# Two parts of the first block's input: from GpSimd's converting loads to SyncE's float32 loads and GpSimd's casts, with w_out's load moved

## The chip, the cores and the metric

The kernel runs on one core of a Trainium2 chip. The core has five engines that run side by side, each with its own instruction queue: TensorE (PE in the profile), VectorE (DVE), ScalarE (ACT), GpSimd (POOL) and SyncE (SP). TensorE loads weights (PEld) and multiplies. SyncE does no arithmetic here; it issues DMA transfers, as ScalarE and GpSimd also can. All transfers run on the core's 16 DMA engines; those that GpSimd issues stand in queue q0 of the profile, those of SyncE in q1. The metric is the device time of one run in microseconds (us).

## The reference

The reference first smooths the input along the sequence with a causal filter of 7 taps, one filter for each of 8 heads with softmax-normalized taps, and then applies a two-layer network with a leaky ReLU:

```python
w = weight - np.max(weight, axis=-1, keepdims=True)          # 8 heads x 7 taps
w = np.exp(w)
w = w / (np.sum(w, axis=-1, keepdims=True) + 1e-09)
x_pad = np.concatenate([np.zeros((B, 6, D)), x], axis=1)     # x: 8 x 4096 x 192
idx = np.arange(S)[:, None] + np.arange(7)[None, :]
x_unf = x_pad[:, idx, :].reshape(B, S, 7, 8, 24)
y = np.einsum('hk,bskhg->bshg', w, x_unf).reshape(B * S, D)  # 32768 x 192
h = y @ w_in                                                 # 192 x 2048
g = np.maximum(0.01 * h, h)
out = g @ w_out                                              # 2048 x 192
```

Inputs and output are float32. The kernel computes with bfloat16 operands.

## The kernel before

The tokens are taken in 32 blocks: a block is 512 positions of two sequences (e = 0 and 1), whose 64-channel chunks lie in the two halves of the partitions. The first two blocks are cut into halves of 256 positions, called groups 0 to 3; from then on a group is a whole block. For a group, the smoothed input yt is made in the layout channels by positions (mostly on DVE: one L222 and six L228 instructions a chunk), TensorE multiplies it with w_in into ph (L507), ScalarE applies the leaky ReLU and writes g (L515), and TensorE multiplies g with w_out (L525 in the first groups, L588 later). The instructions on each engine stand in the order in which the code is written (a manual schedule); waits between engines follow from the tiles that they share.

The channels-by-positions layout needs x transposed. Blocks from 2 on are loaded by GpSimd with conversion to bfloat16 (load_x, L96) and transposed by a DMA that SyncE issues (L114). The four parts (256 positions each) of the first two blocks go other ways, since they are wanted at once:

- Part 0 is loaded in float32 by SyncE (x_nat, L142), cast into x_half by ScalarE and VectorE (cast_first, L155), transposed on TensorE (L181) and copied from there into xt.
- Parts 1 and 2 (called the second and third part) are loaded by GpSimd with conversion into x_rows (load_first, L145), transposed on TensorE (transpose_first, L167; twelve small matmuls that write the tile ptr) and copied into xt by VectorE (evac_first, L195). The first of the two transposes stands in TensorE's order inside group 0's first L507 batch, behind 8 matmuls; the second stands in group 0 ahead of its last batch.
- Part 3 is loaded by GpSimd with conversion into x_half (L149) and transposed by SyncE's DMA (L199).

GpSimd's order of issue before the change: w_in0 for rows 0 to 127; the constant ident; w_in0 for the other 64 rows, in two column halves called near and far, with the two loads of part 1 between them; w_in1 in two loads; the two loads of part 2; w_out in two loads (L350); two small operations that make the filter taps wk (L445, L446), which every L222 and L228 reads; the six loads of part 3; and then the blocks of load_x. w_in's rows are also copied between the halves of the partitions by VectorE and ScalarE (spread_up L326, spread_down L322) before TensorE can use them.

The helper sync adds a wait by hand: its first argument waits for its second. The pool that holds the float32 tile x_nat has two buffers.

Of the kernel before, what the change touches and what calls it, by code (L numbers as in the profile page):

```python
# [10 lines left out]
FP32 = mybir.dt.float32  # L11
BF16 = mybir.dt.bfloat16
# [3 lines left out]
def kernel(  # L16
# [8 lines left out]
    nc = tc.nc  # L25

    B, S, D = x.shape
# [13 lines left out]
    HS = SUB // 2  # L41
    NFC = F // 128
# [3 lines left out]
    RUN = 4  # L46
# [10 lines left out]
    const_pool = ctx.enter_context(tc.tile_pool(name="const", bufs=1))  # L57
    stage_pool = ctx.enter_context(tc.tile_pool(name="stage", bufs=2))
# [17 lines left out]
    x_nat, x_bf, xt = {}, {}, {}  # L76

    def sync(after, first, why):
        tc.add_manual_dep(
            after.ins, first.ins.name,  # L80
            mybir.DependencyInfo(
                mybir.DependencyClass.Sync, mybir.DependencyReason.DATA
            ),
            reason=why,
        )

    def load_x(blk, after=None):

        if blk >= NBLK:
            return  # L90
        rp, st = divmod(blk, NB)
        t = xb_pool.tile([128, NCH, SUB, 2, CH], BF16, name="x_bf")
        src = x[:, st * ST : (st + 1) * ST, :].rearrange("r (s p) d -> r p s d", p=128)
        for c in range(NCH):
            for e in range(2):
                ins = nc.gpsimd.dma_start(  # L96
                    out=t[:, c, :, e, :],
                    in_=src[2 * rp + e, :, :, c * CH : (c + 1) * CH],
                )
                if after is not None:  # L100
                    sync(ins, after, "behind a nearer block's transposes")
                    after = None
        x_bf[blk] = t
# [18 lines left out]
    def new_xt(rp):  # L122
        xt[rp] = xt_pool.tile([128, NCH, HALO + S], BF16, name="xt")
        nc.vector.memset(xt[rp][:, :, 0:HALO], 0.0)
# [8 lines left out]
    x_rows = {  # L133
        q: const_pool.tile([128, 2, HS, D], BF16, name=f"x_rows{q}") for q in (1, 2)
    }

    def load_first(q):
        rows = x[0:2, q * HT : (q + 1) * HT, :].rearrange("e (s p) d -> p e s d", s=HS)
        if q == 0:
            x_nat[q] = stage_pool.tile([128, 2, HS, D], FP32, name="x_nat")  # L140
            for s in range(HS):
                nc.sync.dma_start(out=x_nat[q][:, :, s], in_=rows[:, :, s])  # L142
        elif q in x_rows:
            for e in range(2):
                nc.gpsimd.dma_start(out=x_rows[q][:, e], in_=rows[:, e])  # L145
        else:
            for c in range(NCH):
                for e in range(2):
                    nc.gpsimd.dma_start(  # L149
                        out=x_half[q][:, c, :, e, :],  # L150
                        in_=rows[:, e, :, c * CH : (c + 1) * CH],
                    )

    def cast_first(q, s, copy, e=slice(0, 2)):
        copy(  # L155
            out=x_half[q][:, :, s, e, :],
            in_=x_nat[q][:, e, s, :].rearrange("p e (c k) -> p c e k", c=NCH),
        )
# [76 lines left out]
    def y_of(grp, c):  # L235
        blk, t0, T = grp
        if blk not in yt:
            yt[blk] = yt_pool.tile([128, NCH, ST], BF16, name="yt")
        return yt[blk][:, c, t0 : t0 + T]
# [47 lines left out]
    w9 = const_pool.tile([H, K + 1], FP32, name="w9")  # L287
    nc.scalar.dma_start(out=w9[:, 0:K], in_=weight)  # L288
    load_first(0)

    ones = nc.const_aps.tensor(1.0, [128, ST], BF16)
# [7 lines left out]
    for sign, off in ((1, 0), (-1, GRP - 1)):  # L299
        nc.gpsimd.affine_select(  # L300
            out=sel[:, :, 0, :], in_=sel[:, :, 0, :], compare_op=mybir.AluOpType.is_ge,
# [12 lines left out]
    def load_w_in(n, rows, cols=slice(0, WF)):  # L314
        ps, slot = ((0, 128), 0) if rows == 0 else ((0, CH), 2)
        nc.gpsimd.dma_start(  # L316
            out=w_in[n][ps[0] : ps[1], slot, cols],
            in_=moe_w_in[rows : rows + ps[1], n * WF + cols.start : n * WF + cols.stop],
        )
# [17 lines left out]
    ident = const_pool.tile([128, 128], BF16)  # L337
    make_identity(nc, ident)
    load_w_in(0, 128, near)
    load_first(1)  # L340
    load_w_in(0, 128, far)
    for rows in (0, 128):
        load_w_in(1, rows)
    load_first(2)


    w_out = const_pool.tile([128, NFC, D], BF16)
    for h in range(2):
        cs = slice(h * NFC // (2 * RUN), (h + 1) * NFC // (2 * RUN))
        nc.gpsimd.dma_start(  # L350
            out=w_out.rearrange("p (c i) d -> p c i d", i=RUN)[:, cs],
            in_=moe_w_out.rearrange("(c p i) d -> p c i d", p=128, i=RUN)[:, cs],
        )


    wa = psum_h.tile([128, 2, ST], FP32, name="warm", tag="ph")
# [1 line left out]
    def warm(n, cols=HT, to=wa[:, 0]):  # L358
# [10 lines left out]
        out=nmax, in_=w9[:, 0:K], axis=mybir.AxisListType.X,  # L369
# [3 lines left out]
        out=w9[:, 0:K], in_=w9[:, 0:K], func=mybir.ActivationFunctionType.Exp,  # L373
# [18 lines left out]
    def select(out, parts):  # L392
# [9 lines left out]
    select(wps_hm, slice(0, 2))  # L402
    wps_hm = wps_hm[:, :, 0]
    new_xt(0)
    cast_first(0, 0, nc.scalar.copy)
    cast_first(0, 1, nc.scalar.copy, slice(0, 1))
    cast_first(0, 1, nc.vector.tensor_copy, slice(1, 2))
    taps = const_pool.tile([128, NCH, 2, K + 1, 2], BF16, name="taps")
    nc.vector.tensor_copy(
        out=taps, in_=wps_hm[..., None].to_broadcast([128, NCH, 2, K + 1, 2])  # L410
# [5 lines left out]
    def diag_wide(c, p):  # L416
# [22 lines left out]
        out=rsum, in0=wml[:, :, K:], scalar=1e-9, in1=taps[:, :, 0, K:, 0],  # L439
# [4 lines left out]
    wk = const_pool.tile([128, NCH, K], FP32, name="wk")  # L444
    nc.gpsimd.tensor_add(wk, taps[:, :, 0, 0:K, 0], wml[:, :, 0:K])  # L445
    nc.gpsimd.tensor_mul(wk, wk, rsum.to_broadcast([128, NCH, K]))  # L446
    load_first(3)
    load_x(2)
    diag_wide(1, 1)
# [4 lines left out]
    def act_scale(out, in_, scale):  # L454
# [11 lines left out]
        out=y_of(groups[0], 0), in0=hi[:, :HT], scalar=rsum[:, 0, :], in1=low,  # L466
# [301 lines left out]
```

## Time and profile before

| | |
|---|---|
| median of 3 runs | 680.97 us (680.66 to 681.43) |
| profiled execution, span from its first to its last instruction | 679.2 us |
| what the median has beyond that span | 1.8 us |
| TensorE busy | 674.9 us, 99% of the span, at the full granted clock |
| VectorE, ScalarE, GpSimd busy | 71%, 76%, 22% |
| first L507 matmul | 8.09 us |
| transpose of x's second and third part on TensorE | 8.65 us and 15.98 us |
| first matmul with w_out (L525) | 17.12 us |

The profile gives one execution; its own time is known as the span, and the 1.8 us that the median of the runs has beyond it lie before its first and after its last instruction or are differences between executions. TensorE works almost without a pause from 8.09 us to the end, so the time is decided by what happens ahead of that, by short pauses behind it, and by the amount of TensorE's work, which the change leaves alone. In lists of instructions a line reads: start, duration, engine, line of the code, operation, output tile <- input tiles, count, and in brackets the idle time ahead of it with what ended it.

### The profile page before, as it was taken

The numbers are of one execution on the slowest core, as the hardware profiler recorded it, in microseconds if no ns is written. First come the engines' busy times: TensorE is split into PE (matmuls) and PEld (weight loads), VectorE is DVE, ScalarE is ACT, GpSimd is POOL, SyncE is SP. The second block draws the span as 40 slices with busy tenths as digits, with TensorE's granted clock in tenths as the row PEclk, the third lists the DMA queues.
The fourth block names the chain that finished last, engine by engine and source line by source line (L and its number), as shares of the span: only waits on it lengthen the run. The fifth ranks groups of instructions, "written<-read, shape, count | busy, mean of one in ns | idle before, by whom it ended". The sixth has DMA issues, their size and how long they took to land.

```text
span 679.2 us, 27092 instructions
## 1 busy us (share of the span) xinstructions
PE 674.9 (99%) x12442; PEld 446.3 (66%) x12442; DVE 481.2 (71%) x816; ACT 517.6 (76%) x601; POOL 147.4 (22%) x208
## 2 busy tenths in 40 slices
PE   9999999999999999999999999999999999999998
PEld 6997666666666666666666666666666666666667
DVE  7989477866768766778667687667786676876612
ACT  7899877777787777777777777778777777777781
POOL 8455221122211222211222112222022220000000
PEclk9999999999999999999999999999999999999999
DMA  9999755655737656556556566567365573321123
GB/s 149 99 119 104 52 85 83 84 64 67 96 74 93 76 54 86 84 85 86 66 63 92 80 92 78 56 83 94 73 87 69 60 96 71 72 56 33 34 49 94
DMA packets 213970, 53.27 MB, mean 78 GB/s; under 512 B 209312, under 2 KB 213536, under 8 KB 213856
## 3 DMA queue, kind: packets, MB, share of 16 engines
q0 software_dynamic: 98832, 13.97, 30.3%
q1 hardware_dynamic: 115008, 37.57, 28.0%
q8 instruction: 97, 1.59, 0.9%
q14 instruction: 17, 0.14, 0.1%
q10 hardware_dynamic: 16, 0.00, 0.0%
HBM read 28.31 MB, written 25.17 MB: 79 GB/s over the span
## 4 chain that ended last, share of the span: by engine, by line
PE 98%; DVE 1%; ACT 0%; issue 0%; ACTq 0%
PE ph L507 49%; PE acc L588 44%; PE po L525 5%; PE acc L259 0%; DVE diag L420 0%; PE ptr L167 0%; ACT L366 0%; ACTq L288 0%; DVE w_in L322 0%; DVE yt L465 0%; DVE o_sb L638 0%; DVE x_half L155 0%; ACT w L372 0%; DVE w_in L326 0%; ACT junk L366 0%
## 5 line engine op out<-in xcount | busy, mean ns | idle before, releaser
L515 ACT ACTIVATE g<-ph 128x1024 bf16<-128x1024 f32 x512 | 496.6, 1021 | 139.8 <-PE ph L507 139.6
L228 DVE SCALAR_TENSOR_TENSOR yt<-xt,wk,yt 128x512 bf16<-128x512 bf16 (+1 forms) x582 | 380.1, 715 | 0.2
L507 PE MATMUL ph<-yt,w_in 64*64 64x512 bf16 (+2 forms) x6048 | 377.5, 369 | 0.3 <-DVE yt L465 0.3
L588 PE MATMUL acc<-g,w_out 64*64 64x512 bf16 x5568 | 339.9, 376 | 0.0
L507 PEld LDWEIGHTS <-w_in 64*64 64x64 bf16 (+1 forms) x6048 | 229.7, 131 | 103.4 <-issue 1.1
L588 PEld LDWEIGHTS <-w_out 64*64 64x64 bf16 x5568 | 178.2, 118 | 118.8
L96 POOL DMA_DIRECT2D x_bf<-in_x_dram x180 | 133.9, 774 | 407.6 <-DMA xt<-x_bf 405.6
L610 DVE STREAM_TRANSPOSE o_t<-acc 128x512 f32<-128x512 f32 x87 | 72.9, 875 | 182.2 <-PE acc L588 182.2
L525 PE MATMUL po<-w_out,g 64*128 64x192 bf16 (+1 forms) x640 | 36.8, 243 | 0.0
L525 PEld LDWEIGHTS <-g 64*128 64x128 bf16 (+1 forms) x640 | 32.6, 95 | 3.2 <-issue 0.4
L222 DVE TENSOR_SCALAR yt<-xt,wk 128x512 bf16<-128x512 bf16 (+1 forms) x97 | 28.8, 320 | 2.4 <-DMA xt<-x_bf 2.4
L598 ACT COPY junk<-junk 128x1 f32<-128x1 f32 x58 | 11.1, 191 | 4.1
L638 DVE COPY o_sb<-po 128x192 f32<-128x192 f32 x8 | 2.8, 356 | 6.8 <-PE po L525 3.9
L638 ACT COPY o_sb<-po 128x192 f32<-128x192 f32 x16 | 5.1, 323 | 0.3
L259 PE MATMUL acc<-xt,diag 64*64 64x256 bf16 x126 | 4.7, 272 | 0.1
L149 POOL DMA_DIRECT2D x_half<-in_x_dram x6 | 4.3, 732 | 0.9 <-DMA w_in<-in_moe_w_in_dram 0.9
L259 PEld LDWEIGHTS <-diag 64*64 64x64 bf16 x140 | 3.7, 106 | 1.0 <-issue 0.4
L360 PE MATMUL warm<-const-bfloat16-1.0 128*128 128x512 bf16 (+2 forms) x8 | 3.3, 577 | 0.8 <-PEq L752 0.8
L145 POOL DMA_DIRECT2D x_rows<-in_x_dram x4 | 2.9, 746 | 0.0
L316 POOL DMA_DIRECT2D w_in<-in_moe_w_in_dram x5 | 2.9, 593 | 0.0
L360 PEld LDWEIGHTS <-const-bfloat16-1.0 128*128 128x128 bf16 x10 | 1.2, 128 | 2.2 <-issue 2.2
L326 DVE COPY w_in<-w_in 64x512 bf16<-64x512 bf16 (+1 forms) x7 | 2.3, 337 | 0.2
(52 smaller groups left out, 25.9 us busy)
## 6 DMA issues: line engine op xcount, KB each, us to landing
out_dram<-o_t SPq DMA_DIRECT2D x112, 192.0 KB, 4.7
x_bf<-in_x_dram POOLq DMA_DIRECT2D x180, 64.0 KB, 3.1
out_dram<-o_sb SPq DMA_DIRECT2D x8, 192.0 KB, 2.8
xt<-x_bf SPq DMA_TRANSPOSE x90, 3.2
w_out<-in_moe_w_out_dram POOLq DMA_DIRECT2D x2, 384.0 KB, 8.3
out_dram<-o_t SPq DMA_DIRECT2D x8, 96.0 KB, 2.4
out_dram<-o_sb SPq DMA_DIRECT2D x8, 96.0 KB, 1.7
w_in<-in_moe_w_in_dram POOLq DMA_DIRECT2D x2, 256.0 KB, 5.5
```

Source lines behind the costliest of these rows:

```text
L96: ins = nc.gpsimd.dma_start(out=t[:, c, :, e, :], in_=src[2 * rp + e, :, :, c * CH : (c + 1) * CH],)
L222: lambda s=src, d=dst, c=c: nc.vector.tensor_scalar_mul(d, s, wk[:, c, 0:1])
L228: lambda s=src, d=dst, c=c, k=k: nc.vector.scalar_tensor_tensor(out=d, in0=s, scalar=wk[:, c, k : k + 1], in1=d, op0=mybir.AluOpType.mult, ...
L259: lambda k=k, p=p, a=a, ps=ps, to=to, acc=accs[e]: nc.tensor.matmul(out=acc[to, :T], lhsT=diag[c][ps, p, k, :], rhs=xt[0][ps, c, a : a + T ...
L360: nc.tensor.matmul(out=to[:, 0:cols], lhsT=ones[:, 0:128], rhs=ones[:, 0:cols], start=True, stop=True,)
L507: nc.tensor.matmul(out=ph[m : m + M, e, i * T : (i + 1) * T], lhsT=w_in_of(f, e, c, m, m + M), rhs=y[ps, c, t0 : t0 + T], start=(c == chun ...
L515: act = nc.scalar.activation(out=g[blk][:, nf * u : nf * (u + 1), :, t0 : t0 + T], in_=ph.rearrange("p e (i t) -> p i e t", i=nf), func=my ...
L525: return nc.tensor.matmul(out=po[m], lhsT=g[b][ps, fc, e, s * 128 : (s + 1) * 128], rhs=w_out[ps, fc, :], start=start, stop=stop,)
L588: ins = nc.tensor.matmul(out=acc2[gi, r][e * CH : (e + 1) * CH, 0:T], lhsT=w_out_of(ps, fc, r), rhs=g[b][ps, fc, e, t0 : t0 + T], start=fi ...
L598: seal = nc.scalar.copy(out=junk, in_=junk)
L610: nc.vector.transpose(out=osb[gi, 0][:, 0 : T // GB, :, r], in_=acc2.pop((gi, r))[:, 0:T].rearrange("p (j k) -> p j k", k=GB),)
L638: ins = copy(out=o_sb[:, n % 2, :], in_=po.pop(n))
```

## The change

The second and the third part of x are no longer loaded with conversion by GpSimd. SyncE loads each in float32 into a tile x_nat, in two transfers, and GpSimd casts each into x_rows with two copies. SyncE's loads of the second part wait for ScalarE's first cast of part 0; those of the third part wait for GpSimd's second cast of the second part. On GpSimd, w_out's two loads now stand behind the casts of the second part, and ahead of everything of the third; wk's two operations follow, then the casts of the third part, then the loads of part 3 and of the blocks as before. What TensorE, VectorE and ScalarE execute, and its order, is the same in both kernels. SyncE has four more loads ahead of its first DMA transpose.

```diff
--- before.py
+++ after.py
@@ -134,12 +134,18 @@
         q: const_pool.tile([128, 2, HS, D], BF16, name=f"x_rows{q}") for q in (1, 2)
     }
 
-    def load_first(q):
+    def load_first(q, after=None):
         rows = x[0:2, q * HT : (q + 1) * HT, :].rearrange("e (s p) d -> p e s d", s=HS)
         if q == 0:
             x_nat[q] = stage_pool.tile([128, 2, HS, D], FP32, name="x_nat")
             for s in range(HS):
                 nc.sync.dma_start(out=x_nat[q][:, :, s], in_=rows[:, :, s])
+        elif q in (1, 2):
+            x_nat[q] = stage_pool.tile([128, 2, HS, D], FP32, name="x_nat")
+            for e in range(2):
+                ins = nc.sync.dma_start(out=x_nat[q][:, e], in_=rows[:, e])
+                if e == 0:
+                    sync(ins, after, "behind a nearer part")
         elif q in x_rows:
             for e in range(2):
                 nc.gpsimd.dma_start(out=x_rows[q][:, e], in_=rows[:, e])
@@ -152,7 +158,7 @@
                     )
 
     def cast_first(q, s, copy, e=slice(0, 2)):
-        copy(
+        return copy(
             out=x_half[q][:, :, s, e, :],
             in_=x_nat[q][:, e, s, :].rearrange("p e (c k) -> p c e k", c=NCH),
         )
@@ -337,20 +343,9 @@
     ident = const_pool.tile([128, 128], BF16)
     make_identity(nc, ident)
     load_w_in(0, 128, near)
-    load_first(1)
     load_w_in(0, 128, far)
     for rows in (0, 128):
         load_w_in(1, rows)
-    load_first(2)
-
-
-    w_out = const_pool.tile([128, NFC, D], BF16)
-    for h in range(2):
-        cs = slice(h * NFC // (2 * RUN), (h + 1) * NFC // (2 * RUN))
-        nc.gpsimd.dma_start(
-            out=w_out.rearrange("p (c i) d -> p c i d", i=RUN)[:, cs],
-            in_=moe_w_out.rearrange("(c p i) d -> p c i d", p=128, i=RUN)[:, cs],
-        )
 
 
     wa = psum_h.tile([128, 2, ST], FP32, name="warm", tag="ph")
@@ -402,9 +397,20 @@
     select(wps_hm, slice(0, 2))
     wps_hm = wps_hm[:, :, 0]
     new_xt(0)
-    cast_first(0, 0, nc.scalar.copy)
+    after = cast_first(0, 0, nc.scalar.copy)
+    load_first(1, after)
     cast_first(0, 1, nc.scalar.copy, slice(0, 1))
     cast_first(0, 1, nc.vector.tensor_copy, slice(1, 2))
+    for e in range(2):
+        gate = nc.gpsimd.tensor_copy(out=x_rows[1][:, e], in_=x_nat[1][:, e])
+    w_out = const_pool.tile([128, NFC, D], BF16)
+    for h in range(2):
+        cs = slice(h * NFC // (2 * RUN), (h + 1) * NFC // (2 * RUN))
+        nc.gpsimd.dma_start(
+            out=w_out.rearrange("p (c i) d -> p c i d", i=RUN)[:, cs],
+            in_=moe_w_out.rearrange("(c p i) d -> p c i d", p=128, i=RUN)[:, cs],
+        )
+    load_first(2, gate)
     taps = const_pool.tile([128, NCH, 2, K + 1, 2], BF16, name="taps")
     nc.vector.tensor_copy(
         out=taps, in_=wps_hm[..., None].to_broadcast([128, NCH, 2, K + 1, 2])
@@ -444,6 +450,8 @@
     wk = const_pool.tile([128, NCH, K], FP32, name="wk")
     nc.gpsimd.tensor_add(wk, taps[:, :, 0, 0:K, 0], wml[:, :, 0:K])
     nc.gpsimd.tensor_mul(wk, wk, rsum.to_broadcast([128, NCH, K]))
+    for e in range(2):
+        nc.gpsimd.tensor_copy(out=x_rows[2][:, e], in_=x_nat[2][:, e])
     load_first(3)
     load_x(2)
     diag_wide(1, 1)
```

## The prediction

> **What bounds the kernel now.** I read the page's busy times first, then the chain that ended last, then its first microseconds, then the DMA packets.
>
> ```profile
> PE 674.9 (99%) x12442; PEld 446.3 (66%) x12442; DVE 481.2 (71%) x816; ACT 517.6 (76%) x601; POOL 147.4 (22%) x208
> ...
> PE 98%; DVE 1%; ACT 0%; issue 0%; ACTq 0%
> ```
>
> TensorE is dense: 98% of the chain is PE. The only room is the ramp ahead of the first L507 matmul at 8.09 us and a few short gaps behind it. The chain in order of time shows the place that the change touches:
>
> ```profile
> 7.56 0.49 DVE yt L465
> 8.05 0.04 issue
> 8.09 0.63 PE ph L507 x8
> 8.72 0.46 PE ptr L167 x12
> 9.18 1.00 PE ph L507 x16
> 10.18 0.78 PE acc L259 x24
> 10.96 1.44 PE ph L507 x24
> 12.40 0.67 PE acc L259 x20
> ```
>
> "PE ptr L167" at 8.72 (its weight load at 8.65) is the transpose of x's second part, x_rows1. It stands in PE's order between two batches of L507, so if x_rows1 isn't there, PE waits, and everything after it is already dense. So each microsecond that x_rows1 comes after 8.65 is a microsecond of the run. How early it comes is a matter of the DMA queues:
>
> ```profile
> x_rows<-in_x_dram POOLq DMA_DIRECT2D x2, 96.0 KB, 3.8
> ...
> q1 hardware_dynamic: 371, 0.27, 100.1%
> ...
> q0 software_dynamic: 89, 0.17, 99.0%
> ...
> q1 hardware_dynamic: 129, 0.10, 65.8%
> q0 software_dynamic: 151, 0.02, 48.9%
> ```
>
> The first line: GpSimd's two loads of x_rows1, issued at 3.62 and about 4.35, land at about 7.5 and 8.05, so there are 0.6 us to spare. The others are packets by queue in four stretches. From 2.4 to 3.2 us SyncE's queue q1 is alone with float32 rows of x: 371 packets in 0.8 us on 16 engines, 34.5 ns of one engine each. From 4 to 5 us GpSimd's q0 is alone with w_in: 89 packets in 1 us, 180 ns each. The last two lines are one stretch (32.2 to 32.8 us) in which both queues have work: 129 packets of 768 bytes against 151 of 128 bytes. Nearly one for one: the engines take turns by packets, not by bytes or time. That is the finding that I build on, because the change puts small packets of x (768 bytes) against large ones of w_in (2 KB written) and of w_out (1.5 KB).
>
> **The change part by part.**
>
> *GpSimd's x_rows issues go (4, 0.72 to 0.77 us each).* w_in's last three loads are asked for 1.44 us earlier (from 3.6 instead of 5.03). The wait that this could save is DVE's 0.61 us at 12.21 for w_in1, behind which PE's 24 matmuls at 13.07 take 1.68 us instead of 1.31 to 1.44: at most 0.4 us for PE. GpSimd then has nothing to issue from about 5.3 us until the casts.
>
> *x part 2 on SyncE.* Its first load waits for ScalarE's first cast (L155, 3.44 to 3.95), so it is issued at about 4.0 and the second 0.45 us later (x_nat: 0.45 us an issue). Part 1 was issued at 0.81 and its first packet came at 1.85; 1.04 us on from 4.0 is 5.04. Each load is 256 packets, 16 an engine; 32 in all. At 5.04, by the packet counts, 123 of w_in0's 128 packets have gone; left ahead on q0 are near and far (4 an engine each, half as large, estimated 90 ns), w_in1's 8 of 180 and 4 more of 180. One for one: near and far take 8 x (90 + 34.5) = 1.0 us, w_in1's eight 8 x 214.5 = 1.7, and the first load is through at 7.75. The next four take 0.86 (8.6); then q0 is empty, for w_out has not been asked for, and the last 12 take 0.41: 9.0 us. From an average engine's last packet to the landing was 0.4 us for x_nat and about 0.9 for x_rows1, where a slow engine lags; I take the middle: landing at 9.65. Bounds: 9.4 and 10.0; if time were shared equally, 2 x 1.1 us from 5.04 and the 0.4, 7.6.
>
> The page on the DMA of the Trainium skill ("DMA: Bandwidth & Descriptors", section on queues, rings and completion order) says that an engine drains a whole packet of typically 9 to 17 descriptors from one ring before it turns to the next. Were that so for x's rows, its 32 would wait for some 3 turns of w_in only, land at about 7.2, and the transpose would find its data; the sum would then be no loss at all. The stretch of 129 against 151 speaks for the smaller turns, and I go by it.
>
> *The casts on GpSimd (2 + 2).* Not in the trace: GpSimd has no copy of 128x384. Its memsets of 128 and 192 columns take 228 and 258 ns (0.47 ns a column, 0.35 us for 384); its affine selects 287 and 355 (1.06 a column, 0.56 us). A cast reads as the select does, so 0.5 us, bounds 0.35 and 0.6. The first is hidden behind the wait for the second load. The second is on the path: x_rows1 is ready at 9.65 + 0.5 = 10.15. PE stalls from 8.65: **1.5 us**. Early end, with packets in turns: 9.4 + 0.35, 1.1 us. Late end: 10.0 + 0.6 and 0.5 behind a VectorE instruction, 2.4. With time shared equally: 7.6 + 0.35, no stall.
>
> One row hints at such blocking: the copy L326 at 9.88 takes 0.36 us where its five likes of 64x512 take 0.29, and it ran beside GpSimd's L446. The page "SBUF — State Buffer" (who interferes with whom) has it that GpSimd and a VectorE instruction of two SBUF inputs or a two-port mode exclude each other for a whole instruction; by it a cast could wait up to the 0.5 us of an L228. The row shows 0.07 us. At 9.65 VectorE would itself be waiting for the transposes, so I put nothing on the first pair.
>
> *w_out behind the casts, ahead of x part 3.* Before: issued at 8.05 and 8.8, landed at 15.8 and 17.6; PE wants the halves at 17.12 and 19.09. After: issued 2.1 us later, but q0 carries neither of x's parts (x_rows took 243 packets in 0.6 us, 40 ns each, 64 an engine, 2.5 us), and PE asks 1.5 us later. Nothing. GpSimd's wk (L445, L446: 0.63 us) stands behind these issues and the casts: 10.15 + 1.48 + 0.63 = 12.3, where DVE's L222 would want it at 10.26 + 1.5 = 11.75. So DVE waits 0.5 us for wk in place of its 0.6 for w_in1: the possible gain of 0.4 is given back, I count zero.
>
> *x part 3.* Its load waits for the second cast: issued at T = 10.15, first packet T + 1.04, against w_out's packets from T + 1.46 (109 ns each: 147 in the microsecond from 14). Some 3 go before; 29 x (109 + 34.5) = 4.2 us; landed by T + 6.3, cast by T + 6.8. PE wants it at 15.98, which is 8.65 + 7.33, now T + 7.33. Covered by 0.5 us: zero; if the lag is 0.9 and each cast waits behind an L228, up to 0.8.
>
> *Queued behind part 3's casts on GpSimd:* the six x_half3 loads (0.73 us each), before at 10.09 to 15.35, now from about T + 6.8 = 17 to 21.4, then SP's transposes L199. q0 is empty by then, so with x_bf's 2.8 us the last loads land at 23.5 and the third transpose (4.7 to 5.2 us to landing) at 28.4; DVE wants it at 26.84 + 1.5 = 28.3. Just covered. It matters because DVE has no slack up to 46 us:
>
> ```profile
> 35.48 10.67 DVE L228 SCALAR_TENSOR_TENSOR yt<-xt,wk,yt 128x512 bf16<-128x512 bf16 x16
> ...
> 46.21 1.29 PE ph L507 x12
> ```
>
> DVE ends block 2's convolution at 46.15, and PE's first matmuls on it run from 46.21: what DVE loses before that beyond about 0.3 us, PE loses too.
>
> **Sum.** 1.5 + 0 + 0 - 0 = 1.5 us on the profiled span of 679.2, which lies 1.8 us below the median of 680.97: 680.97 + 1.5 = 682.4 to 682.5; I say 682.4.
>
> **Rivals.** Forecast (x part 2 is late; from 1.1 us with 0.2 of the gain kept, 681.9, to 2.4 with 0.2 lost elsewhere, 683.6): 0.58, since 129 against 151 speaks for it, though no stretch shows packets as large as w_in's on the other side.
>
> Not slower: SyncE's packets get equal time or more. Landed at 7.6, cast at 8.1, ready before 8.65; w_in1 comes early and wk is in time, so DVE's 0.61 goes and PE wins up to 0.4: 680.6 to 681.2. It decides if x part 2 lands before 8.15. For it: packets of both queues overlap in an engine (65.8 + 48.9% is over 100%). 0.27.
>
> Much slower: beside the stall, GpSimd's second pair of casts is held up behind DVE's back-to-back L228 (0.5 us each), part 3 is late at PE by up to 0.8, and x_half3 comes late at DVE by 1 more, which PE pays at 46 us: 1.5 + 0.8 + 0.7 = 3.0, 683.6 to 685. 0.12.
>
> Faster by over 0.2% (1.36 us, about what a measurement can tell from no change): the gaps behind 8.09 hold 0.4 us and the ramp ahead isn't touched, so only something unseen: 0.03.
>
> The range reaches from the second case to over the forecast's end: 680.6 to 683.9, leaving out most of the third and the last. About two thirds of the forecast's chance (0.39), the third case and a little for the unseen lie above 1.36 us: slower 0.53; same 0.44; faster 0.03.
>
> **What would show it.** Right: PE idle before the L167 line near 8.7 for 1 to 2 us, put down to GpSimd's cast, which itself waited for x_nat; x_nat's landings over 4 us instead of 2.6; DVE waiting for wk rather than w_in1; no new gap at 46 us. Wrong: x_nat's loads landing within 3 us; casts of over 0.7 us; or PE's wait at 16 rather than 8.7 us.

## The result and the profile after

The changed kernel takes 685.58 us (685.06 to 686.45, 5 runs), against 681.24 (680.66 to 681.46, 5 runs) for the kernel before on the same chip: +4.34 us, a ratio of 1.0068 with a 95% interval of 1.0056 to 1.0080. It is slower, as forecast, but by almost three times the 1.5 us of the sum, and outside the range. The profiled execution took 686.45 us with a span of 684.7, 5.5 more than the span before; the other four runs have spans of 683.3 to 684.1.

In the code of the changed kernel the L507 matmuls stand at L515, the transposes of x_rows (L167) at L173, L525 at L533, VectorE's L222 and L228 at L228 and L234, its copies L326 at L332; GpSimd's casts are L405 (part 2) and L454 (part 3). Here, as for most of the prediction, part 2 and part 3 are the second and the third part of x, which go through x_rows; the first keeps the name part 0 (the prediction's "Part 1 was issued at 0.81" is this one), and the fourth goes by its tile, x_half.

From the page: TensorE is still at 99% and still 98% of the chain, but its busy time has risen from 674.9 to 678.1 us for the same 12442 matmuls. That is the first sign that something beside a wait has come in.

```profile
PE 678.1 (99%) x12442; PEld 450.5 (66%) x12442; DVE 480.5 (70%) x816; ACT 517.9 (76%) x601; POOL 146.6 (21%) x208
...
PE 98%; DMA 1%; POOL 0%; ACT 0%; DVE 0%; issue 0%; POOLq 0%
...
x_nat<-in_x_dram SPq DMA_DIRECT2D x6, 192.0 KB, 3.9
```

The chain of work that ended last, in order of time (start, duration, what). Before, the transposes stood at 8.72 and nothing but TensorE followed; now the chain starts with x's second part:

```profile
4.03 6.28 DMA x_nat<-in_x_dram
...
10.37 0.50 POOL x_rows L405
...
10.88 0.52 POOL x_rows L405
...
11.44 0.85 PE ptr L173 x11
12.29 1.83 PE ph L515 x16
14.12 1.42 PE acc L265 x24
15.54 2.42 PE ph L515 x24
17.96 0.67 PE acc L265 x20
18.63 1.43 PE ph L515 x24
```

The first load takes 6.28 us to land, both casts follow one another, and the transposes come at 11.44: 2.7 us late. But the rows behind it are dearer too: 16 matmuls of L515 took 1.00 us before and 1.83 here, and 24 of them 1.44 and 2.42. Busy times in stretches show why (start and end, length, busy time with instructions by engine, and in the column behind POOL the granted TensorE clock). The first line is of the kernel before, the others of the changed kernel:

```profile
14.00:16.00 2.00, 2.00 (x39) 1.41 (x35) 1.90 (x5) 1.87 (x2) 1.35 (x2) 1.00 1.22 201
...
9.00:10.00 1.00, 0.00 (x0) 0.00 (x0) 0.00 (x0) 0.37 (x1) 0.00 (x0) 1.00 0.80 191
10.00:11.00 1.00, 0.08 (x1) 0.08 (x1) 0.00 (x0) 0.00 (x0) 0.62 (x2) 0.87 0.14 35
14.00:16.00 2.00, 2.00 (x32) 1.31 (x32) 1.89 (x6) 1.02 (x1) 0.50 (x1) 0.50 1.13 234
17.00:18.00 1.00, 1.00 (x16) 0.62 (x16) 0.93 (x3) 1.00 (x1) 1.00 (x2) 0.72 0.94 167
18.00:20.00 2.00, 2.00 (x46) 1.60 (x43) 0.44 (x1) 1.57 (x3) 2.00 (x4) 1.00 0.39 32
```

In the changed kernel TensorE has nothing to do from 8.70 to 10.92. Near 10.7 the granted clock falls to 0.50; it stays there until after 17 us. Before, it was 1.00 throughout. From the transposes to the first matmul with w_out took 8.57 us before (8.72 to 17.29) and 11.17 here (11.44 to 22.61): 2.7 us of the 5.5 are the late start and 2.6 the rows behind it: the transposes and the 64 matmuls that follow them take 2.8 us longer at half clock, and 0.25 comes back where 24 matmuls had waited for w_in1 (1.68 us before, 1.43 here). Little is lost behind 22.6.

The packets by queue while part 2 is under way, 5.7 to 11 us, and below them from 6 to 9 us, when both queues have work throughout:

```profile
q0 software_dynamic: 323, 0.47, 54.0%
q1 hardware_dynamic: 544, 0.39, 25.7%
...
q0 software_dynamic: 233, 0.36, 71.7%
q1 hardware_dynamic: 365, 0.27, 31.0%
```

The 323 packets of q0 took 54% of 5.3 us = 2.9 us of each engine. 56 of them are under 512 bytes, so some 17 large ones an engine went; the sum had 20 (near, far and w_in1), also at 2.9 us. From 6 to 9 us 1.6 packets of x's queue went for one of w_in's: not one for one, and far from the 3.5 for one that equal time would give at 40 ns and 142 ns a packet (25.7% and 54.0% of 5.3 us over 34 and 20 packets an engine).

The second load was issued at 4.44 and landed 6.4 us later, at 10.8, only 0.5 us behind the first:

```profile
4.44 0.47 SPq L146 DMA_DIRECT2D x_nat<-in_x_dram x1
...
x_nat<-in_x_dram SPq DMA_DIRECT2D x1, 192.0 KB, 6.4
```

### The profile page after: what moved, and what is told of

The parts are those of the page before. It is cut to its first block, busy times and chain, and to the rows that moved or that the text cites. A ratio compares the mean times of both kernels' runs of the same rounds, so it can differ in the third digit from the quotient of the medians.

```text
span 684.7 us, 27098 instructions
## 1 busy us (share of the span) xinstructions
PE 678.1 (99%) x12442; PEld 450.5 (66%) x12442; DVE 480.5 (70%) x816; ACT 517.9 (76%) x601; POOL 146.6 (21%) x208
## 4 chain that ended last, share of the span: by engine, by line
PE 98%; DMA 1%; POOL 0%; ACT 0%; DVE 0%; issue 0%; POOLq 0%
PE ph L515 49%; PE acc L596 44%; PE po L533 5%; DMA x_nat<-in_x_dram 1%; PE acc L265 0%; PE ptr L173 0%; POOL x_rows L405 0%; ACT x_half L161 0%; DVE o_sb L646 0%; POOLq L452 0%
## 5 line engine op out<-in xcount | busy, mean ns | idle before, releaser
L234 DVE SCALAR_TENSOR_TENSOR yt<-xt,wk,yt 128x512 bf16<-128x512 bf16 (+1 forms) x582 | 381.5, 726 | 0.2
L515 PE MATMUL ph<-yt,w_in 64*64 64x512 bf16 (+2 forms) x6048 | 379.2, 370 | 0.1
L515 PEld LDWEIGHTS <-w_in 64*64 64x64 bf16 (+1 forms) x6048 | 230.7, 131 | 103.7 <-issue 1.3
L596 PEld LDWEIGHTS <-w_out 64*64 64x64 bf16 x5568 | 180.9, 119 | 116.5
L533 PE MATMUL po<-w_out,g 64*128 64x192 bf16 (+1 forms) x640 | 36.8, 243 | 0.0
L533 PEld LDWEIGHTS <-g 64*128 64x128 bf16 (+1 forms) x640 | 32.6, 95 | 3.2 <-issue 0.4
L228 DVE TENSOR_SCALAR yt<-xt,wk 128x512 bf16<-128x512 bf16 (+1 forms) x97 | 29.3, 328 | 3.1 <-DMA xt<-x_bf 2.9
L173 PE MATMUL ptr<-ident,x_rows 128*64 128x128 bf16 x24 | 1.7, 269 | 2.4 <-POOL x_rows L405 2.4
L173 PEld LDWEIGHTS <-x_rows 128*64 128x64 bf16 x24 | 1.1, 135 | 3.1 <-POOL x_rows L405 2.9
```

Source lines behind the costliest of these rows:

```text
L228: lambda s=src, d=dst, c=c: nc.vector.tensor_scalar_mul(d, s, wk[:, c, 0:1])
L234: lambda s=src, d=dst, c=c, k=k: nc.vector.scalar_tensor_tensor(out=d, in0=s, scalar=wk[:, c, k : k + 1], in1=d, op0=mybir.AluOpType.mult, ...
L515: nc.tensor.matmul(out=ph[m : m + M, e, i * T : (i + 1) * T], lhsT=w_in_of(f, e, c, m, m + M), rhs=y[ps, c, t0 : t0 + T], start=(c == chun ...
L533: return nc.tensor.matmul(out=po[m], lhsT=g[b][ps, fc, e, s * 128 : (s + 1) * 128], rhs=w_out[ps, fc, :], start=start, stop=stop,)
L596: ins = nc.tensor.matmul(out=acc2[gi, r][e * CH : (e + 1) * CH, 0:T], lhsT=w_out_of(ps, fc, r), rhs=g[b][ps, fc, e, t0 : t0 + T], start=fi ...
```

## The experiments

My theory after this look: the loss is the stall at part 2 (2.7 us) plus the time at half clock which the stall brings on (1.4 us in most runs, where the mean clock is 0.998 as the view rounds it: 0.002 x 684). The rival: the clock matters little, and what goes beyond the 1.5 us comes from later, from part 3, w_out, wk or the x_half loads that now stand behind the casts. Twelve runs followed: ten other kernels, the changed kernel once more, and one of the ten a second time. "Transposes" is when the last eleven or twelve of part 2 start in the profiled execution (8.72 before); the clock is that execution's mean.

| kernel | median, us | ratio, 95% interval | transposes | span, clock |
|---|---|---|---|---|
| changed | 685.58 | 1.0068 (1.0056 to 1.0080) | 11.44 | 684.7, 0.995 |
| changed, again | 685.90 | 1.0073 (1.0060 to 1.0087) | 11.5 | 683.3, 0.998 |
| TensorE's gap filled | 685.75 | 1.0068 (1.0053 to 1.0082) | 11.52 | 682.7, 1.0 |
| part 3 only | 685.45 | 1.0071 (1.0054 to 1.0089) | as before | 683.5, 0.998 |
| part 2's loads without wait | 684.45 | 1.0051 (1.0039 to 1.0063) | 9.62 | 682.7, 1.0 |
| w_in1 behind the casts | 683.33 | 1.0037 (1.0025 to 1.0049) | 9.06 | 683.1, 0.998 |
| part 2 only | 687.26 | 1.0091 (1.0078 to 1.0104) | 14.56 | 686.6, 0.995 |
| filled, x_half ahead | 685.31 | 1.0066 (1.0054 to 1.0078) | 12.17 | 683.3, 1.0 |
| the same, again | 686.19 (1 run) | | 12.57 | 684.5, 1.0 |
| without wait, x_half ahead | 682.67 | 1.0024 (1.0015 to 1.0033) | 9.19 | 680.6, 0.999 |
| x_half ahead | 685.78 | 1.0071 (1.0059 to 1.0083) | 11.86 | 683.9, 0.998 |
| before, with a stall | 685.21 | 1.0064 (1.0052 to 1.0077) | 11.49 | 684.4, 0.995 |
| before, stall filled | 683.71 | 1.0038 (1.0025 to 1.0050) | 11.71 | 682.0, 1.0 |

### What a stall costs by itself, with and without the low clock

Two variants of the kernel before leave all loads as they were. In the first, TensorE's first transpose of part 2 waits for two useless copies on ScalarE, placed to end where the changed kernel's data comes. In the second, 36 useless transposes of ident fill that wait.

```diff
+    for _ in range(2):
+        late = nc.scalar.copy(out=idle_out, in_=idle_in)
...
+                    if q == 1 and (s, c, e) == (0, 0, 0):
+                        sync(ins, late, "a stall of known length")
```

The second has this besides, ahead of those transposes:

```diff
+            for _ in range(36 if q == 1 else 0):
+                nc.tensor.transpose(out=t[:, 0, 0, :], in_=ident, identity=ident)
```

> The kernel before, with a stall of known length put at the place in question: ScalarE does two useless copies (128x1024) behind its L322 copy, where it otherwise waits for TensorE, and the first transpose of x part 2 waits for the second of them. All transfers are as in the kernel before. ScalarE ends them at about 11.4 us, so TensorE stands idle from 8.7 to 11.4. Theory (a stall of this length costs itself plus a low clock behind it): 2.7 us of stall and 1.4 to 3.4 us of low clock, 684.5 to 687, with a mean granted clock of 0.998 or 0.995. Rival (the clock has no price that is seen in the time): 683.3 to 684.

> The same stall in the kernel before, with the 36 useless transposes of ident on TensorE ahead of the first transpose of x part 2 (2.2 us of TensorE work inside the stall). Theory: the clock stays at 1.00 and only the stall of 2.7 us is left: 683.3 to 684.2, 1.4 to 3 us under the run without the filling. Rival (the filling buys nothing, as the near equal times of the changed kernel with and without it, 685.75 and 685.58, could be read): the same time as without it.

The stretches from 11 to 14 and from 14 to 17 us, first of the stall alone:

```profile
11.00:14.00 3.00, 2.51 (x28) 1.66 (x28) 1.52 (x5) 1.46 (x2) 2.38 (x4) 0.50 1.23 183
14.00:17.00 3.00, 3.00 (x40) 1.97 (x40) 2.82 (x8) 1.02 (x1) 1.70 (x3) 0.50 1.46 188
```

then of the filled stall:

```profile
11.00:14.00 3.00, 2.29 (x54) 1.81 (x56) 1.62 (x5) 2.04 (x3) 2.30 (x4) 1.00 1.26 186
14.00:17.00 3.00, 3.00 (x64) 2.52 (x62) 2.85 (x7) 2.55 (x4) 1.88 (x3) 1.00 1.45 192
```

The clock, third from the right, is 0.50 in the one and 1.00 in the other: in the three microseconds from 14 TensorE does 40 matmuls or 64. The medians are 685.21 and 683.71 us: the low clock costs 1.50 us and the delay itself 2.42. The filled run's transposes even started 0.2 us later (11.71 against 11.49), so 1.50 is not too much. With no load moved at all, an idle TensorE at this place brings the time to within 0.4 us of the changed kernel's. So a stall of this length is enough for the size of the loss, and in this kernel 1.5 us of it is the clock. Whether the changed kernel loses it in the same two terms is a matter of its own runs.

### The changed kernel with its gap filled

The same 36 transposes in the changed kernel:

```diff
+            for _ in range(36 if q == 1 else 0):
+                nc.tensor.transpose(out=t[:, 0, 0, :], in_=ident, identity=ident)
```

> The changed kernel with 36 more TensorE instructions: transposes of the constant ident into the tile that the transposes of x part 2 overwrite, put just ahead of these in TensorE's order, so that TensorE works (about 2.2 us) through the gap from 8.7 to 10.9 us instead of standing idle. They do no useful work. Theory (the loss of 4.3 us is a stall of 2.7 us until x part 2 is there, and then a granted clock of 0.50 for some microseconds because TensorE had been idle): x part 2 comes no earlier, the transposes start at 11.0 to 11.4, but the clock stays at 1.00 and the 16 matmuls behind take 1.0 us instead of 1.83: 683.6 to 684.2, about 1.5 us under the changed kernel. Rival (the matmuls behind the stall are slow because their operands or PSUM are contended by GpSimd's casts and the DMAs, not by the clock): the slow stretch stays, 685.3 to 686.

The clock stayed at 1.00, and the matmuls behind the stall went at their old speed, so the profiled span fell to 682.7; the 16 matmuls behind the transposes, from TensorE's timeline (start, duration):

```profile
11.97 1.06 PE L517 MATMUL ph<-yt,w_in 64*128 64x256 bf16 x16
```

The median did not fall: 685.75. The six runs lie between 684.14 and 688.08, five of them at a clock of 1.000, so something else varies between executions. The kernels with the x_half loads ahead, below, show a part of what it is.

### Why part 2 lands so late

w_in1's two loads moved behind the casts of part 2:

```diff
-    for rows in (0, 128):
-        load_w_in(1, rows)
...
         gate = nc.gpsimd.tensor_copy(out=x_rows[1][:, e], in_=x_nat[1][:, e])
+    for rows in (0, 128):
+        load_w_in(1, rows)
```

> The changed kernel with w_in1's two loads moved on GpSimd from ahead of the casts of part 2 to behind them, ahead of w_out. Part 2's loads then meet near and far only. Theory (w_in1's packets hold part 2 back): part 2 lands at 7.6 to 8.3 instead of 10.3 and 10.9, is cast by 8.4 to 9.0, the stall at 8.7 falls from 2.2 to under 0.4 us and the clock stays at 1.00; but w_in1 is then asked for at about 9 and lands at 11.5 to 13.5, where VectorE wants it at 12.2, and w_out comes 1.3 us later: 681 to 682.5. Rival (part 2 is late because of SyncE's late start and the lag of slow engines, whatever else is queued): landing after 9.5, 684 and more.

The chain in order of time, and below it a line of TensorE's timeline (start, duration, count, and in brackets the idle time ahead of it):

```profile
3.99 4.10 DMA x_nat<-in_x_dram
...
8.15 0.50 POOL x_rows L403
...
9.74 5.48 DMA w_in<-in_moe_w_in_dram
```

```profile
14.93 0.64 PE L515 MATMUL ph<-yt,w_in 64*128 64x256 bf16 x4 [1.05 <-DVE w_in L332]
```

With w_in1 gone from q0, part 2's load lands after 4.10 us instead of 6.28, and the transposes start at 9.06. So w_in1's packets held it, which is the prediction's mechanism. The bytes have to come some time: now w_in1 is late, at 15.23, and TensorE waits 1.05 us for it ahead of 14.93, and 0.16 us once more. Four of the five runs, at 0.999 or 1.0, have spans of 681.4 to 681.8; the one at 0.998 has 683.1. In that profile the clock is at 0.50 from 16.1 to 19.5 us: these short waits brought it down once in five runs.

Part 2's change alone (part 3 stays with GpSimd):

```diff
-        elif q in (1, 2):
+        elif q == 1:
...
         load_w_in(1, rows)
+    load_first(2)
```

> Part 3 of x as in the kernel before (two converting loads by GpSimd behind w_in1, no SyncE loads, no casts); only part 2 by SyncE in float32 with GpSimd's casts, and w_out behind these casts. Theory (part 2 by itself makes the stall at 8.7 us, and the clock falls behind it; part 3 adds a second loss through x_half3, which is hidden while the first is larger): a stall of 2 to 3.5 us (x part 3's packets now also take turns with part 2's), then the clock at 0.50 for 2 to 7 us in most runs: 684 to 685.8, about as the changed kernel. Rival (most of the loss comes with part 3, as the run with part 3 alone, 685.45, could be read): 681.5 to 683.

Its second load took 9.55 us and TensorE idled 3.87 and 1.72 us; the half of the change costs more than the whole (687.26), which fits that part 3's packets on q0 now also stand beside part 2's:

```profile
4.40 9.55 DMA x_nat<-in_x_dram
```

Part 3's change alone, its loads asked for after wk's first operation and behind w_out:

```diff
-        elif q in (1, 2):
+        elif q == 2:
...
+    gate = nc.gpsimd.tensor_add(wk, taps[:, :, 0, 0:K, 0], wml[:, :, 0:K])
+    load_first(2, gate)
```

> Part 2 of x as in the kernel before (two converting loads by GpSimd between near and far); only part 3 by SyncE in float32 with GpSimd's casts, its loads waiting for GpSimd's first wk operation, behind w_out's loads. Theory (all of the loss comes with part 2): no stall at 8.7, part 3 is cast by about 14.5 to 15.5 us, ahead of the 15.98 at which TensorE wants it: 680.6 to 681.4, the same as before within 0.3 us. Rival (part 3, with w_out's packets against it, or the loads of x_half3 that stand behind its casts on GpSimd, costs by itself): 681.8 to 683.

```profile
8.87 9.07 DMA x_nat<-in_x_dram
...
18.00 0.52 POOL x_rows L452
...
18.56 0.85 PE ptr L173 x11
```

Against w_out's packets the load took 9.07 us, TensorE idled 1.37 and 0.65 us ahead of the second transposes, and the clock was 0.53 from 18 to 20. So in this place part 3 costs as much as the whole change. In the changed kernel TensorE reaches the second transposes only at 21.38 and doesn't wait for them: part 2's lateness has moved everything that needs part 3. My theory, that this half would be near free, missed.

Part 2's loads without the wait for ScalarE's cast (asked for right behind part 0's):

```diff
-    load_first(1, after)
+    load_first(1)
```

> The changed kernel without the wait of part 2's loads for ScalarE's first cast: SyncE issues them at about 1.7 and 2.2 us, right behind part 0. Theory (part 2 is late because it starts when w_in's packets are queued and then gets one packet for each of theirs): it starts at about 3.5 when part 0 is through, shares the engines with w_in0, lands at 5.5 to 6.5, is cast by 7.5, and no stall is left at 8.7; w_in0 comes 0.5 to 1 us later than its 6.4 and moves VectorE's first copy of it (6.73) and the first L507 by 0 to 0.8 us. Time 680.6 to 681.8. Rival (SyncE's loads in float32 are slow by themselves): landing later than 8, a stall of over 0.5 us, 682 and more.

Part 2 lands at 7.5 and 8.3, there is no stall at it and no fall of the clock, but 684.45 us is still 3.4 too many. 1 us of it is w_in0: its packets now share with x's, the first L515 starts at 9.06 instead of 8.09. The rest lies where nothing had been lost in the changed kernel, shown by a line each from the timelines of VectorE and TensorE:

```profile
30.18 0.29 DVE L228 TENSOR_SCALAR yt<-xt,wk 128x256 bf16<-128x256 bf16 x1 [1.70 <-DMA xt<-x_half]
```

```profile
48.92 0.41 PE L515 MATMUL ph<-yt,w_in 64*128 64x512 bf16 x2 [1.81 <-DVE yt L234]
```

VectorE waits 0.83 and 1.70 us for x_half, and TensorE pays 1.81 us when it reaches block 2 near 49 us. The prediction had called these loads "just covered"; with TensorE back at its pace they aren't.

### The second loss, hidden behind the first

The six x_half loads moved ahead of part 3's casts, in the changed kernel, in the one without wait, and in the filled one:

```diff
+    load_first(3)
     for e in range(2):
         nc.gpsimd.tensor_copy(out=x_rows[2][:, e], in_=x_nat[2][:, e])
-    load_first(3)
```

> The changed kernel with only x_half3's loads moved ahead of part 3's casts on GpSimd. Theory (stall and low clock push TensorE so far back that x_half3 is in time anyway): 685.0 to 686.0, the same as the changed kernel within 0.5 us; the difference to the run that has the filling as well is the price of the low clock, 1.3 to 2.6 us. Rival (the changed kernel's loss is x_half3's in the main): 682.5 to 684.

> The changed kernel without the wait of part 2's loads for ScalarE's first cast, and with x_half3's loads ahead of part 3's casts on GpSimd. Theory: in the run without that wait the stall had gone to the start (w_in0 landed 1.3 us later, since x took turns with it, and the first L507 came 1.3 to 1.4 us later) and TensorE lost 2.06 us near 48 us to x_half3; the second goes, the first stays: 681.8 to 682.8. Rival (x_half3's order does not matter): 684 to 685.

> The changed kernel with the 36 filling transposes on TensorE, and with the six loads of x_half3 moved on GpSimd from behind part 3's casts to ahead of them. Theory (in the run with the filling alone the clock stayed at 1.00, but a second loss showed that had been hidden: GpSimd waits 2 to 2.6 us for part 3, x_half3 is asked for 7 us later than before, its transposes land at about 30, VectorE waits and TensorE waits for VectorE near 48 us): with both taken away only the stall of 2.7 us at 8.7 is left: 683.2 to 684.2, and no wait of VectorE for xt<-x_half. Rival (the second loss is VectorE's own work being slowed, not x_half3): 685 to 686 as with the filling alone.

In the changed kernel it gives nothing (685.78 against 685.58 and 685.90): its x_half loads are hidden behind the stall and the low clock. Without the wait it gives 1.8 us (684.45 to 682.67), and TensorE's pause near 47 is down to this:

```profile
47.42 1.27 PE L515 MATMUL ph<-yt,w_in 64*128 64x512 bf16 x10 [0.16 <-DVE yt L234]
```

This is the best variant, and it is still slower than the kernel before, by 0.24% (0.15 to 0.33). Its chain goes back to the second load of part 0, which part 2's loads now follow at once. It took 3.21 us instead of 2.63, and the first L515 starts at 8.63 instead of 8.09:

```profile
1.32 3.21 DMA x_nat<-in_x_dram
```

In the filled kernel no wait for x_half was left, and yet 685.31 us came, not 683.2 to 684.2. It was therefore profiled a second time.

> The kernel with 36 filling transposes and the x_half loads asked for ahead of part 3's casts, profiled a second time. If filling TensorE's gap goes with a later landing of part 2, the second load lands at 11.0 us or later again and the transposes of part 2 start at 12.0 us or later, as in its first profile (12.17 us); the span is then 683 us or more at a clock of 0.999 or 1.0. If the late landing was one execution's chance, the transposes start near 11.5 us, as in the changed kernel, and the span is 681.5 to 682.7 us at that clock.

Part 2 landed late again (casts at 10.96 and 12.01, transposes at 12.57; span 684.5 at clock 1.0), as the first of the two expectations had it. The chain of that execution tells more. It leaves TensorE altogether and runs on VectorE up to 51 us:

```profile
12.01 0.51 POOL x_rows L407
12.51 1.38 POOL w_out L411 x2
...
14.23 0.23 POOL wk L454
...
14.48 0.30 DVE yt L230
...
40.68 10.60 DVE yt L236 x16
...
51.33 1.27 PE ph L517 x10
```

Behind the casts GpSimd issues w_out (1.38 us) before wk; VectorE waits 0.42 us for wk; and from there its convolution has no slack up to block 2. Its last sixteen instructions for that block started at 35.48 before and start at 40.60 in VectorE's timeline here, 5.1 us late; the span is 5.3 longer. In the filled kernel without the move the pair is 3.4 and 3.5, and its chain too runs on VectorE up to block 2 (in its case by way of a 0.53 us wait for x_half). In the first profile of the filled kernel with the move it is 3.9 and 4.1; there the chain leaves VectorE earlier, at w_in1's copies behind wk. So in these executions filling saves TensorE the slow clock, and then VectorE holds it, late by part 2's landing, by wk and by x_half.

The three profiles of unfilled late landings end in TensorE's own chain. VectorE's lateness there (4.8, 3.6 and 4.0 us) lies 0.5 to 0.7 below the span's excess (5.5, 4.1 and 4.7). That is no bound on what filling could give, for in the two profiles of the changed kernel VectorE itself waits for TensorE's slow matmuls:

```profile
20.55 0.48 DVE L277 TENSOR_SCALAR yt<-acc,rsum 128x256 bf16<-128x256 f32 x1 [2.11 <-PE acc L265]
...
19.25 0.48 DVE L277 TENSOR_SCALAR yt<-acc,rsum 128x256 bf16<-128x256 f32 x1 [0.59 <-PE acc L265]
```

A comparison at the same landing tells more. With the transposes at 11.44 and 11.5 the changed kernel's spans are 684.7 and 683.3; filled, with them at 11.52, the span is 682.7. What the span loses beyond the lateness of the transposes is 1.3 to 2.8 us in the three unfilled profiles and 0.6 to 1.5 in the three filled ones. So the clock costs time in the changed kernel too, and at an equal landing filling gives some of it back. But two of the three filled profiles landed 0.7 to 1.1 us later than the changed kernel, which took the gain away. That fits the equal medians; no run separates how much the landings and how much VectorE have to do with them.

What stays open is the landing's scatter: the second cast started at 10.88 and about 11.0 in the two profiles of the changed kernel, 11.29 with x_half ahead, and about 11.0, 11.6 and 12.0 in the filled ones. Six executions don't tell whether filling has a part in it; no run separates that.

### The changed kernel again

> The changed kernel once more, as it is, beside these two and for a second profile. Theory: 685 to 686.5, part 2's first load landing at 10 to 11 us, TensorE idle from 8.7 until 10.5 to 11.5, then a clock of 0.50 for some microseconds.

```profile
11.54 0.85 PE ptr L173 x11
12.39 1.83 PE ph L515 x16
14.21 0.89 PE acc L265 x23
```

Span 683.3 at 0.998: transposes 2.8 us late, clock 0.50 from 11 to 14 and 0.93 from 14 to 17. The low clock lasts shorter than in the first profile: these three rows take 3.57 us instead of 2.24 before, 1.3 more. 2.8 + 1.3 = 4.1 meets the 4.1 us by which the span is longer.

## Why the prediction was right or wrong

- **Direction and place: right.** TensorE idles ahead of the L167 transposes, put down to GpSimd's cast, which waits for x_nat; chance 0.53 stood on slower.
- **Packets in turns: right in the main.** With equal time part 2 would have landed at 7.6; it landed at 10.8, the packets of q0 beside it took the 2.9 us that the sum gave them (some 17 large ones an engine instead of 20, so each was dearer), and taking w_in1 away brought the landing forward by 2.2 us. The turns weren't one for one (1.6 of x for one of w_in). The page "DMA: Bandwidth & Descriptors" (queues, rings and completion order), weighed in the prediction, has an engine drain 9 to 17 descriptors before it turns. The landing near 7.2 that the prediction worked out from it takes whole packets for x's rows alone; if w_in's queue drains as many at a turn, the 32 rows meet nearly all of w_in's 20 as well. So the landing past 10.3 speaks against that estimate, and doesn't decide between the page and the row of 129 against 151.
- **Size of the stall: 2.7 us, not 1.5.** The landing at 9.65 failed: the second load landed at 10.8. 0.8 of this is the term "first packet at 5.04": 1.04 us was the lead of a load into idle engines, and q1's first packet here came between 5.8 and 5.9. The other 0.4 is the way from the first packet to the landing, 5.0 us instead of 4.6. 1.5 + 0.8 + 0.4 = 2.7. The first load was expected through at 7.75 and landed at 10.31; why it came so close to the second is open. It cost nothing more, for its cast was over at 10.87, when the second load had only just landed. The cast's own 0.5 us was exact.
- **The step that was missing: the clock.** The sum took a stall to cost its length. TensorE's rows behind it were priced at full clock, though nothing in the trace of before showed what an idle TensorE does to it. It cost 1.3 us in the second profile of the changed kernel, 2.8 in the first, and 1.50 in the kernel before with the stall (with and without filling). 1.5 + 1.2 + 1.3 to 1.5 is 4.0 to 4.2 of the 4.34 us measured. That filling alone didn't bring the changed kernel's median down is explained only in part (above).
- **w_out, wk, part 3: zero, right in the changed kernel, but not for the reason given.** w_in1's wait went as predicted, and the wait for wk that was to take its place, 0.5 us, was 0.41 to 0.42 in four other profiles. In the changed kernel's own chain they cost nothing, for the later stall and the slow clock cover them; part 3's change by itself costs 0.71%, and in the filled kernel wk behind w_out holds VectorE.
- **x_half "just covered": wrong, without effect on the time.** 1.8 us of loss stood ready near 48 us and showed as soon as part 2 was on time.
- **The rivals.** "Not slower" fell with the landing. "Much slower" gave the nearest time (683.6 to 685), but by part 3 and x_half, which the changed kernel doesn't pay. None had the clock.

## What to carry to other kernels

Before pricing a stall of a busy TensorE, add what its clock does afterwards: here 2.7 us of waiting went with a loss of 4.3, and in the kernel before a run with the gap filled by useless work, beside one with nearly the same stall unfilled, told the two terms apart. When a transfer moves to another queue, count the packets still queued elsewhere and their time, and take the lead of a first packet from a load issued into busy engines. A second path that is "just covered" is only covered as long as the first loss stands: undoing the first showed the second, and mending both still left the shared engines to pay for.

## What the runs showed of the hardware

- The granted clock fell to 0.50 after 2.2 to 2.8 us without TensorE work in both profiles of the changed kernel and in that of the stall in the kernel before; all ten runs of the changed kernel have a mean clock of 0.995 or 0.998. It also fell behind shorter waits: 1.37 us (part 3 only), 1.37 and 0.85 (x_half ahead), 1.05 and 0.16 (w_in1 behind the casts, one run of five); it did not behind 1.35 us ahead of the first L515 (part 2's loads without wait), so the length of the wait alone doesn't decide it here. The low clock lasted 6.8 us in three profiles (the first of the changed kernel: 10.73 to 17.56) and 3.4 in four (the second: 11.0 to 14.4). The Trainium skill's page "TensorE: Matmul & The Clock Gate" (Part 1) has half rate after an idle window of about 3.4 us and full rate after as long a busy one. Half rate and the length agree; a shorter idle time sufficed here.
- The same 192 KB load of x landed 2.66 us after its issue on quiet engines (the first load of part 0), 6.28 us beside w_in's packets, and 9.07 us beside w_out's.
